# One value run for each head pair: joining the value products, and the probability adds on one engine

## The chip, the cores and the metric

The kernel runs on one core of a Trainium2 chip. The metric is the device time of one execution in microseconds (us). A time given as "the time before" is the median of three runs; a profile shows one further execution.

## The reference

The computation is a normalised attention, followed by a feed-forward block with a squared relu:

```python
q_n, k_n = rmsnorm(q, g_q), rmsnorm(k, g_k)            # (8, 12, 448, 64) each
scores = (1 / sqrt(64)) * q_n @ k_n.T
attn = exp(scores - max); attn = attn / (sum(attn) + 1e-9)
x = (attn @ v).transpose(0, 2, 1, 3).reshape(3584, 768)
r = maximum(x @ w_in, 0)                               # w_in: (768, 2048)
out = (r * r) @ w_out                                  # w_out: (2048, 768)
```

All of it is float32. There are 8 batches, 12 heads, 448 positions, and 64 numbers to a head.

## The kernel before

The kernel holds two programs and branches on the gains. With these inputs it runs `attention_then_ffn_bounded`, which leaves the maximum out of the softmax, since the scores are bounded.

**Spans.** Two batches make a span, and there are four spans. Two heads make a pair: 6 pairs to a batch, 12 to a span, 48 in all, numbered 0 to 47. A span goes through attention (its 12 pairs), then `first_product` (x times w_in with the squared relu), then `second_product` (times w_out). Both products are done with seven block products in place of eight, on sums and differences of blocks (xC and gC, made on VectorE in `finish` and `combine`).

**Stages, in order of time.** The attention of span 0 (pairs 0 to 11) runs together with the making of the weights, `make_w`: the weights come in as 32-bit words and go through a chain of VectorE (L451), ScalarE (L453, L454), VectorE (L457, L458, L459), ScalarE (L460) and GpSimd (L467, L471 to L474), and are written back to DRAM as blocks (w1s, w2s). Then comes `first_product` of span 0, still with weight making; then three pairs of span 1 "alone" (pairs 12 to 14), with the last of the weights; then, for each span, `second_product` with the attention of the next span woven in: after each half of a pair some matmuls of `second_product` are issued (the "fill"), about 6.5 to a half. The `first_product` of spans 1 to 3 stands by itself between these.

**A pair, as the kernel before issues it.** The generator `attention` gives two halves for each pair i. In the first half it loads q and k of pair i+3, issues `scores(i, 0)` and `scores(i, 1)`, `norm(i + 2)`, then the value products 2 and 3 of pair i-1, and `finish(i - 1)`. In the second half it loads v, issues `transposes(i + 1)`, `scores(i, 2)` and `scores(i, 3)`, then the value products 0 and 1 of pair i. A score product (L561) is one of four blocks of 112 keys, for two heads; ScalarE takes its exponential (L564) into a tile pr. A value product (L582) adds one pr times v into the PSUM tile pav. The row sums (L593, PSUM tile tot) are products with a block of ones. In span 0 and in the three pairs alone every pr is summed that way on TensorE (`pe_sums` true). In the other 33 pairs the four pr are first added into acc, by GpSimd, VectorE and GpSimd in turn (L570, L572), and the ones are multiplied once. `finish` takes the reciprocal of tot (L601), multiplies pav by it (L602) and makes the differences for `first_product`.

**Order.** TensorE and the DMA queue (SyncE) take their instructions in the order in which the code issues them. The order on VectorE, ScalarE and GpSimd is laid out beforehand by a scheduler, so it is fixed when the kernel runs, but is not that of the code.

**Buffers.** PSUM has a pool ps_s with two buffers of two banks (tag s, the scores), a pool ps_o with one buffer each for pav (tag o) and for tot (tag t), and a pool ps_m with two. Tag t of ps_o also holds pa, one of the four accumulators of `first_product`. Tile pr has five buffers, acc one, and v, q and k, and the normed pair have two each.

Of the kernel before, what the change touches and what calls it, by code (L numbers as in the profile page):

```python
# [9 lines left out]
F32 = mybir.dt.float32  # L10
U32 = mybir.dt.uint32
AF = mybir.ActivationFunctionType
ALU = mybir.AluOpType
# [291 lines left out]
def attention_then_ffn_bounded(  # L305
# [34 lines left out]
    nc = tc.nc  # L340

    B, H, S, D = q.shape
    NT, DM = out.shape
    DFF = w_in.shape[1]
    P = 128
    NJ = 4
# [14 lines left out]
    ps_s = ctx.enter_context(tc.tile_pool(name="ps_s", bufs=2, space=bass.MemoryType.PSUM))  # L361
    ps_o = ctx.enter_context(tc.tile_pool(name="ps_o", bufs=1, space=bass.MemoryType.PSUM))
# [147 lines left out]
    qks, vs, qkTs, probs, pavs, tots, accs, normed = {}, {}, {}, {}, {}, {}, {}, {}  # L510

    def load(i):
        b, h0 = i // NPAIR, 2 * (i % NPAIR)
        qk = loads.tile([SP, 2, 2, NJ * D], F32, tag="qk", name="qk")
        for dst, src in ((qk[:, 0], q), (qk[:, 1], k)):
            nc.sync.dma_start(dst, src[b, h0:h0 + 2].rearrange("h (p j) d -> p h (j d)", j=NJ))
        qks[i] = qk

    def load_v(i):
        b, h0 = i // NPAIR, 2 * (i % NPAIR)  # L520
        vs[i] = loads.tile([SP, 2, NJ, D], F32, tag="vt", name="vt")
        nc.sync.dma_start(vs[i].rearrange("p h j d -> p h (j d)"),
                          v[b, h0:h0 + 2].rearrange("h (p j) d -> p h (j d)", j=NJ))
# [20 lines left out]
    def transposes(i):  # L544
        qkn = normed.pop(i)
        qkT = loads.tile([P, 2, S], F32, tag="qkT", name="qkT")
        for s in range(2):
            pt = ps_m.tile([P, S], F32, tag="m", name="pt")
            for j in range(NJ):
                nc.tensor.transpose(pt[:, j * SP:(j + 1) * SP],  # L550
                                    qkn[:, s, j].rearrange("p h d -> p (h d)"), ident[:SP, :SP])
            nc.scalar.activation(qkT[:, s], pt, AF.Copy, scale=gains[:, s:s + 1])  # L552
        qkTs[i] = qkT

    def scores(work, i, c, pe_sums):

        qkT = qkTs[i]
        sc = ps_s.tile([SP, 2, 512], F32, tag="s", name="sc")
        for h in range(2):
            rows = slice(h * D, (h + 1) * D)  # L560
            nc.tensor.matmul(sc[:, h, 0:S], qkT[rows, 1, c * SP:(c + 1) * SP], qkT[rows, 0, :],  # L561
                             start=True, stop=True)
        pr = work.tile([SP, 2, S], F32, tag="pr", name="pr", bufs=5)
        nc.scalar.activation(pr, sc[:, :, 0:S], AF.Exp)  # L564
        probs[i, c] = pr
        if c == 0 or pe_sums:
            pass
        elif c == 1:
            accs[i] = work.tile([SP, 2, S], F32, tag="acc", name="acc", bufs=1)
            nc.gpsimd.tensor_tensor(accs[i], probs[i, 0], pr, ALU.add)  # L570
        else:
            (nc.vector if c == 2 else nc.gpsimd).tensor_tensor(accs[i], accs[i], pr, ALU.add)  # L572
        if c == NJ - 1:
            del qkTs[i]

    def values(i, cs, pe_sums):
        if 0 in cs:
            pavs[i] = ps_o.tile([P, S], F32, tag="o", name="pav")
        for c in cs:
            pr = probs.pop((i, c))  # L580
            for h in range(2):
                nc.tensor.matmul(pavs[i][h * D:(h + 1) * D, :], vs[i][:, h, c, :], pr[:, h, :],  # L582
                                 start=(c == 0), stop=(c == NJ - 1))
            if pe_sums:
                sums(i, pr, c == 0, c == NJ - 1)
        if not pe_sums and NJ - 1 in cs:
            sums(i, accs.pop(i), True, True)

    def sums(i, pr, first, last):
        if first:  # L590
            tots[i] = ps_o.tile([P, S], F32, tag="t", name="tot")
        for h in range(2):
            nc.tensor.matmul(tots[i][h * D:(h + 1) * D, :], ones, pr[:, h, :], start=first, stop=last)  # L593

    def finish(work, i):


        b, hp = divmod(i, NPAIR)
        t = b % 2
        rec = work.tile([P, S], F32, tag="rec", name="rec", bufs=1)  # L600
        nc.vector.reciprocal(rec, tots.pop(i))  # L601
        nc.vector.tensor_tensor(xT[:, t, hp], pavs.pop(i), rec, ALU.mult)  # L602
        del vs[i]
        if t:
            sub = nc.vector.tensor_tensor
            if hp < HC:
                sub(xC[:, 0, hp], xT[:, 1, hp], xT[:, 0, hp], ALU.subtract)
            else:
                n = hp - HC
                sub(xC[:, 1, n], xT[:, 1, hp], xC[:, 0, n], ALU.subtract)  # L610
                sub(xC[:, 2, n], xT[:, 0, hp], xC[:, 1, n], ALU.subtract)
                sub(xT[:, 1, n], xT[:, 1, hp], xT[:, 1, n], ALU.subtract)

    def attention(work, first, end, pe_sums):

        last = (first // (2 * NPAIR) + 1) * 2 * NPAIR
        for i in range(first, end):
            if i + 3 < min(last + 2, B * NPAIR):
                load(i + 3)
            scores(work, i, 0, pe_sums)  # L620
            scores(work, i, 1, pe_sums)
            if i + 2 < last:
                norm(i + 2)
            if i > first:
                values(i - 1, (2, 3), pe_sums)
                finish(work, i - 1)
            yield
            if i + 1 < B * NPAIR:
                load_v(i + 1)
            if i + 1 < last:  # L630
                transposes(i + 1)
            scores(work, i, 2, pe_sums)
            scores(work, i, 3, pe_sums)
            values(i, (0, 1), pe_sums)
            if i == end - 1:
                values(i, (2, 3), pe_sums)
                finish(work, i)
            yield


# [11 lines left out]
    def first_product(work, span):  # L652

        B11, B21, B22 = xT[:, 0, 0:HC], xT[:, 0, HC:], xT[:, 1, HC:]
        T1, T2, T4, T3 = xC[:, 0], xC[:, 1], xC[:, 2], xT[:, 1, 0:HC]

        def product(ps, n, rhs, first):

            load_blocks(n + 5)
            for c in range(HC):  # L660
                nc.tensor.matmul(ps, stream[n][:, c], rhs[:, c], start=first and c == 0,  # L661
                                 stop=c == HC - 1, skip_group_check=not first)

        def activate(g, src):
            nc.scalar.activation(g, src, AF.Relu)  # L665
            if span == 0 and src is not g:
                nc.scalar.activation(g, g, AF.Square)
            else:
                nc.gpsimd.tensor_tensor(g, g, g, ALU.mult)  # L669

        for f in range(HF):
            n = span * (N1 + N2) + f * 7
            g11, g12 = gT[:, f, 0:S], gT[:, f, S:2 * S]
            g21, g22 = gT[:, HF + f, 0:S], gT[:, HF + f, S:2 * S]
            add = nc.vector.tensor_tensor
            pa = ps_o.tile([P, S], F32, tag="t", name="pa")
            product(pa, n + A11, B11, True)
            p1 = work.tile([P, S], F32, tag="p1", name="p1")
            nc.scalar.copy(p1, pa)
            yield  # L680
            pb = ps_m.tile([P, S], F32, tag="m", name="pb")
            product(pb, n + S2, T2, True)
            z = work.tile([P, S], F32, tag="z", name="z")
            add(z, p1, pb, ALU.add)
            yield
            pc = ps_m.tile([P, S], F32, tag="m", name="pc")
            product(pc, n + S1, T1, True)
            y = work.tile([P, S], F32, tag="y", name="y")
            add(y, z, pc, ALU.add)
            yield  # L690
            pd = ps_m.tile([P, S], F32, tag="m", name="pd")
            product(pd, n + S3, T3, True)
            add(g22, y, pd, ALU.add)  # L693
            activate(g22, g22)
            yield
            product(pa, n + A12, B21, False)
            activate(g11, pa)
            yield
            product(pd, n + A22, T4, False)
            add(g21, z, pd, ALU.add)  # L700
            activate(g21, g21)
            yield
            product(pc, n + S4, B22, False)
            add(g12, z, pc, ALU.add)
            activate(g12, g12)
            if span:
                combine(f)
            yield
# [210 lines left out]
```

## Time and profile before

| | |
|---|---|
| time before, median of 3 (lowest, highest) | 1637.28 us (1636.2, 1638.59) |
| profiled execution, its own time | 1638.22 us |
| span of the profiled execution | 1636.4 us |
| TensorE busy | 1521.9 us, 93% of the span |
| VectorE / ScalarE / GpSimd busy | 640.5 / 475.3 / 673.1 us |
| granted TensorE clock, mean | 0.98 |

The span lies 1.8 us under the profiled execution's own time, and this in turn 0.9 us over the median. The stages, by the busy time of each engine in stretches of the span:

| stage | from, to (us) | length | TensorE busy | VectorE busy | GpSimd busy |
|---|---|---|---|---|---|
| start, pair 0 and a part of 1 | 0 to 40 | 40 | 19.3 | 18.2 | 20.4 |
| attention of span 0, weights | 40 to 204 | 164 | 127.8 | 108.9 | 123.9 |
| first product of span 0, weights | 204 to 326 | 122 | 120.5 | 67.6 | 73.1 |
| its end, pairs 12 to 14 alone, pair 15 | 326 to 411 | 85 | 69.6 | 58.9 | 63.8 |
| second product 0 with attention | 411 to 612 | 201 | 191.7 | 67.7 | 74.4 |
| first product 1 | 612 to 740 | 128 | 127.6 | 41.3 | 33.8 |
| second product 1 with attention | 740 to 989 | 249 | 238.4 | 91.5 | 115.9 |
| first product 2 | 989 to 1117 | 128 | 127.6 | 41.3 | 33.9 |
| second product 2 with attention | 1117 to 1366 | 249 | 238.5 | 89.3 | 104.0 |
| first product 3, second product 3 | 1366 to 1636 | 270 | 261.0 | 55.9 | 29.9 |

How to read the profile's lines: PE is TensorE, PEld its weight loads, DVE VectorE, ACT ScalarE, POOL GpSimd, SP SyncE. A line of the timeline gives the start and the length in us, the engine, the line of the kernel, the operation, the tiles written and read, their shapes, and the count of records; a bracket at the end gives the idle time ahead of it and what ended it. Each float32 matmul leaves two records, so that the value products of one pr for two heads are 4 records. "Issue" as the one that ended a wait means that the profile shows no releaser.

### The profile page before, as it was taken

The numbers are of one execution on the slowest core, as the hardware profiler recorded it, in microseconds if no ns is written. First come the engines' busy times: TensorE is split into PE (matmuls) and PEld (weight loads), VectorE is DVE, ScalarE is ACT, GpSimd is POOL, SyncE is SP. The second block draws the span as 40 slices with busy tenths as digits, with TensorE's granted clock in tenths as the row PEclk, the third lists the DMA queues.
The fourth block names the chain that finished last, engine by engine and source line by source line (L and its number), as shares of the span: only waits on it lengthen the run. The fifth ranks groups of instructions, "written<-read, shape, count | busy, mean of one in ns | idle before, by whom it ended". The sixth has DMA issues, their size and how long they took to land.

```text
span 1636.4 us, 14479 instructions
## 1 busy us (share of the span) xinstructions
PE 1521.9 (93%) x5172; PEld 709.1 (43%) x5172; DVE 640.5 (39%) x729; ACT 475.3 (29%) x661; POOL 673.1 (41%) x516
## 2 busy tenths in 40 slices
PE   4778799978999999999999999999999999999998
PEld 2233244533444445554444445554444445555544
DVE  4666846576323233333334342333333342332001
ACT  5455535463222301123332311122332321111000
POOL 5966746686344411235555421225455420221000
PEclk9798999989999999999999999999999999999999
DMA  5355467874232223322332313333222213333332
GB/s 169 103 158 169 134 221 245 257 225 126 67 102 79 85 69 100 99 87 85 91 95 85 97 57 98 88 98 97 85 83 89 79 52 96 87 87 93 103 106 64
DMA packets 157717, 180.37 MB, mean 110 GB/s; under 512 B 10692, under 2 KB 134084, under 8 KB 157636
## 3 DMA queue, kind: packets, MB, share of 16 engines
q1 hardware_dynamic: 157636, 179.35, 36.5%
q8 instruction: 43, 0.70, 0.2%
q14 instruction: 38, 0.31, 0.1%
HBM read 146.28 MB, written 33.03 MB: 110 GB/s over the span
## 4 chain that ended last, share of the span: by engine, by line
PE 82%; DVE 4%; POOL 4%; ACT 3%; issue 3%; DMA 3%; SPq 1%; POOLq 0%; DVEq 0%; ACTq 0%
PE ps L733 32%; PE pa L661 8%; PE sc L561 8%; PE pav L582 8%; PE pd L661 8%; PE pc L661 8%; PE pb L661 4%; PE tot L593 3%; PE pt L550 2%; ACT qkT L552 1%; DMA qk<-in_k_dram 1%; POOL qkn L537 1%; DVE ct L747 1%; POOL gC L467 1%; DMA w2s<-gC 1%
## 5 line engine op out<-in xcount | busy, mean ns | idle before, releaser
L733 PE MATMUL ps<-gT,sw 128*128 128x448 f32 x768 | 306.6, 547 | 7.1 <-DVE ct L747 3.6
L669 POOL TENSOR_TENSOR gT<-gT 128x448 f32<-128x448 f32 x120 | 115.2, 961 | 376.2 <-ACT gT L665 376.2
L733 PE MATMUL ps<-gC,sw 128*128 128x448 f32 x576 | 232.3, 549 | 4.0 <-ACT osb L725 2.0
L601 DVE RECIPROCAL rec<-tot 128x448 f32<-128x448 f32 x48 | 141.9, 2956 | 236.2 <-PE tot L593 236.2
L564 ACT ACTIVATE pr<-sc 112x896 f32<-112x896 f32 x192 | 166.6, 913 | 191.7 <-PE sc L561 191.7
L582 PE MATMUL pav<-pr,vt 112*64 112x448 f32 x768 | 180.4, 579 | 42.1 <-issue 34.6
L733 PEld LDWEIGHTS ps<-gT,sw 128*128 128x128 f32 x768 | 141.0, 190 | 157.3 <-issue 140.7
L561 PE MATMUL sc<-qkT 64*112 64x448 f32 x768 | 173.5, 570 | 6.9 <-ACT pr L564 6.0
L661 PE MATMUL pa<-xT,sw 128*128 128x448 f32 x384 | 157.2, 546 | 3.1 <-DVE rec L601 3.1
L733 PEld LDWEIGHTS ps<-gC,sw 128*128 128x128 f32 x576 | 106.8, 191 | 119.3 <-issue 111.5
L535 POOL TENSOR_TENSOR rstd<-rstd,mhalf 112x16 f32<-112x16 f32 x48 | 140.1, 2919 | 3.8
L665 ACT ACTIVATE gT<-gT 128x448 f32<-128x448 f32 x96 | 55.1, 575 | 291.8 <-DVE gT L693 183.3
L534 POOL TENSOR_SCALAR rstd<-rstd 112x16 f32<-112x16 f32 x48 | 32.8, 682 | 245.0 <-DVE rstd L533 244.1
L582 PEld LDWEIGHTS pav<-pr,vt 112*64 112x64 f32 x768 | 50.6, 142 | 154.8 <-issue 148.5
L725 ACT COPY osb<-po 112x512 f32<-112x512 f32 x48 | 28.1, 586 | 279.2 <-PE po L723 279.2
L552 ACT ACTIVATE qkT<-pt,gains 128x448 f32<-128x448 f32 x96 | 58.7, 632 | 172.9 <-PE pt L550 172.9
L537 POOL TENSOR_TENSOR qkn<-qk,rstd 112x512 f32<-112x512 f32 x96 | 104.3, 1108 | 3.6
L661 PEld LDWEIGHTS pa<-xT,sw 128*128 128x128 f32 x384 | 73.4, 192 | 74.6 <-issue 70.8
L570 POOL TENSOR_TENSOR acc<-pr 112x896 f32<-112x896 f32 x33 | 70.5, 2136 | 84.9 <-PE tot L593 79.3
L533 DVE TENSOR_REDUCE rstd<-qkn 112x16 f32<-112x1024 f32 x48 | 58.2, 1212 | 116.2 <-ACT qkn L530 115.9
L561 PEld LDWEIGHTS sc<-qkT 64*112 64x112 f32 x768 | 61.4, 174 | 88.2 <-issue 65.7
L550 PE MATMUL pt<-ident,qkn 112*128 112x112 f32 x384 | 53.5, 270 | 37.5 <-ACT qkT L552 16.7
(82 smaller groups left out, 1651.6 us busy)
## 6 DMA issues: line engine op xcount, KB each, us to landing
sw<-w1s SPq DMA_DIRECT2D x224, 192.0 KB, 2.4
sw<-w2s SPq DMA_DIRECT2D x168, 256.0 KB, 2.7
qk<-in_q_dram SPq DMA_DIRECT2D x48, 224.0 KB, 3.3
qk<-in_k_dram SPq DMA_DIRECT2D x48, 224.0 KB, 3.7
vt<-in_v_dram SPq DMA_DIRECT2D x48, 224.0 KB, 3.0
w1s<-gC SPq DMA_DIRECT2D x8, 1344.0 KB, 6.1
w2s<-gC SPq DMA_DIRECT2D x24, 448.0 KB, 4.5
out_dram<-osb SPq DMA_DIRECT2D x48, 224.0 KB, 2.9
```

What stands on the lines that cost most here:

```text
L535: nc.gpsimd.tensor_tensor(rflat, rflat, mhalf, ALU.pow)
L537: nc.gpsimd.tensor_tensor(qkn[:, s].rearrange("p j h d -> p h j d"), qk[:, s].rearrange("p h (j d) -> p h j d", d=D), rstd[:, s].rearrange ...
L550: nc.tensor.transpose(pt[:, j * SP:(j + 1) * SP], qkn[:, s, j].rearrange("p h d -> p (h d)"), ident[:SP, :SP])
L552: nc.scalar.activation(qkT[:, s], pt, AF.Copy, scale=gains[:, s:s + 1])
L561: nc.tensor.matmul(sc[:, h, 0:S], qkT[rows, 1, c * SP:(c + 1) * SP], qkT[rows, 0, :], start=True, stop=True)
L564: nc.scalar.activation(pr, sc[:, :, 0:S], AF.Exp)
L570: nc.gpsimd.tensor_tensor(accs[i], probs[i, 0], pr, ALU.add)
L582: nc.tensor.matmul(pavs[i][h * D:(h + 1) * D, :], vs[i][:, h, c, :], pr[:, h, :], start=(c == 0), stop=(c == NJ - 1))
L601: nc.vector.reciprocal(rec, tots.pop(i))
L661: nc.tensor.matmul(ps, stream[n][:, c], rhs[:, c], start=first and c == 0, stop=c == HC - 1, skip_group_check=not first)
L669: nc.gpsimd.tensor_tensor(g, g, g, ALU.mult)
L733: nc.tensor.matmul(ps, stream[n][:, c % 4], rhs_of[i][:, c], start=c == 0, stop=c == HF - 1)
```

## The change

All four value products of a pair, and the row sums, are issued in one run right behind the score products 2 and 3 of the same pair, and `finish` follows at once. The first half of a pair keeps only its two score products. In the 33 pairs that add the pr tiles, all three adds are on VectorE. The accumulator pa of `first_product` moves out of the tag t of ps_o into the two buffers of ps_s. Each line of the kernel after L564 stands some lines higher, by up to 9 (L601 becomes L597, L602 L598, L733 L724); below, the numbers are those of the kernel before.

```diff
         nc.scalar.activation(pr, sc[:, :, 0:S], AF.Exp)
         probs[i, c] = pr
-        if c == 0 or pe_sums:
-            pass
-        elif c == 1:
+        if c == 1 and not pe_sums:
             accs[i] = work.tile([SP, 2, S], F32, tag="acc", name="acc", bufs=1)
-            nc.gpsimd.tensor_tensor(accs[i], probs[i, 0], pr, ALU.add)
-        else:
-            (nc.vector if c == 2 else nc.gpsimd).tensor_tensor(accs[i], accs[i], pr, ALU.add)
+        if c and not pe_sums:
+            nc.vector.tensor_tensor(accs[i], probs[i, 0] if c == 1 else accs[i], pr, ALU.add)
...
-    def values(i, cs, pe_sums):
-        if 0 in cs:
-            pavs[i] = ps_o.tile([P, S], F32, tag="o", name="pav")
-        for c in cs:
+    def values(i, pe_sums):
+        pavs[i] = ps_o.tile([P, S], F32, tag="o", name="pav")
+        for c in range(NJ):
...
-        if not pe_sums and NJ - 1 in cs:
+        if not pe_sums:
             sums(i, accs.pop(i), True, True)
...
             scores(work, i, 1, pe_sums)
             if i + 2 < last:
                 norm(i + 2)
-            if i > first:
-                values(i - 1, (2, 3), pe_sums)
-                finish(work, i - 1)
             yield
...
             scores(work, i, 2, pe_sums)
             scores(work, i, 3, pe_sums)
-            values(i, (0, 1), pe_sums)
-            if i == end - 1:
-                values(i, (2, 3), pe_sums)
-                finish(work, i)
+            values(i, pe_sums)
+            finish(work, i)
             yield
...
-            pa = ps_o.tile([P, S], F32, tag="t", name="pa")
+            pa = ps_s.tile([P, 2, 512], F32, tag="s", name="pa")[:, 0, 0:S]
```

## The prediction

> **What bounds the kernel now.** I read the busy shares first, then the waits of TensorE stage by stage, then the timeline where it waits.
>
> ```profile
> PE 1521.9 (93%) x5172; PEld 709.1 (43%) x5172; DVE 640.5 (39%) x729; ACT 475.3 (29%) x661; POOL 673.1 (41%) x516
> ```
>
> TensorE bounds the whole; a change that leaves its work alone can win only its idle time and its slow clock. By stage, idle is 36 us of 164 in span 0's attention (40 to 204), some 15 at 326 to 411, about 10 in each later attention stage, nothing in `first_product`. The waits of TensorE up to 204:
>
> ```profile
> PE pav L582 <- issue: 25.4, 10, 3.5
> PE pt L550 <- POOL qkn L537: 15.8, 1, 15.8
> PE pav L582 <- DVE xT L602: 7.4, 1, 7.4
> ```
>
> So 32.8 us are spent ahead of value product 0, in 11 places. What it waits for shows in one such place (timeline):
>
> ```profile
> 116.05 0.92 PE L593 MATMUL tot<-pr,ones 112*64 112x448 f32 x4
> ...
> 117.82 1.76 PE L561 MATMUL sc<-qkT 64*112 64x448 f32 x8
> 118.21 2.95 DVE L601 RECIPROCAL rec<-tot 128x448 f32<-128x448 f32 x1
> 121.25 1.22 DVE L533 TENSOR_REDUCE rstd<-qkn 112x16 f32<-112x1024 f32 x1
> 122.38 0.61 DVE L602 TENSOR_TENSOR xT<-pav,rec 128x448 f32<-128x448 f32 x1
> 123.10 1.76 PE L582 MATMUL pav<-pr,vt 112*64 112x448 f32 x4 [3.52 <-issue]
> ```
>
> pav has one buffer. It is free once VectorE has taken the reciprocal and multiplied: some 6 us after the sums, while TensorE has only 0.92 us of transposes and 1.7 of scores to put in between. Then the clock: these 4 records take 1.76 us, others 0.97. The end of this stage has the same wait, on tag t:
>
> ```profile
> 201.55 2.96 DVE L601 RECIPROCAL rec<-tot 128x448 f32<-128x448 f32 x1 [1.01 <-PE tot L593]
> 204.54 0.62 DVE L602 TENSOR_TENSOR xT<-pav,rec 128x448 f32<-128x448 f32 x1
> 204.57 4.85 PE L661 MATMUL pa<-xT,sw 128*128 128x448 f32 x6 [3.05 <-DVE rec L601]
> ```
>
> In the 33 pairs woven into `second_product` there is a fill between the sums and value product 0, so no such wait. What the change touches there (timeline, one second half):
>
> ```profile
> 827.35 1.72 ACT L564 ACTIVATE pr<-sc 112x896 f32<-112x896 f32 x2
> 827.46 1.72 PE L582 MATMUL pav<-pr,vt 112*64 112x448 f32 x8
> 827.49 1.22 DVE L533 TENSOR_REDUCE rstd<-qkn 112x16 f32<-112x1024 f32 x1 [2.31 <-ACT qkn L530]
> 828.62 1.08 DVE L572 TENSOR_TENSOR acc<-acc,pr 112x896 f32<-112x896 f32 x1
> ```
>
> **What the Trainium skill says.** "TensorE: Matmul & The Clock Gate", "Part 1: The HAM clock gate": after an idle window the array runs at half clock until some 3.4 us of work have passed. The trace agrees (1.76 for 0.97; pa 4.85 us, later 2.25), and about half of the 11 waits show it. "GPSIMD Engine Reference", 3.1: an elementwise add costs VectorE about 1 cycle an element, GpSimd 2.6; here the same add takes 1.08 and 2.08 us. "SBUF — State Buffer", "SBUF: two separate sides": VectorE with two SBUF inputs and GpSimd exclude each other for an instruction. Agreed: GpSimd's small L534 takes 0.97 us beside the add at 809.5, otherwise 0.20.
>
> **The change part by part.**
>
> *Span 0, pairs up to 4: -0.9.* VectorE is busy nearly without a gap from 26.7 to 52.8 with weights, GpSimd from 39.7 to 86.7; VectorE then waits 7.4 and 5.5 us for weight words. The word load issued at 76.2 stands on SyncE behind a q, k load that waits for GpSimd's `norm` (74.7). The change moves none of this; I carry the chain word load, L451, L453, L454, L457, reciprocal, L602 through in the new order, and value product 0 of pair 4 comes at 94.7 in place of 95.6.
>
> *Pairs 4 to 11: -11.2.* The first value product goes from 95.59 to 193.71, seven periods of 14.02 us. TensorE's own work in one is 3.4 (scores) + 0.9 (transposes) + 6.3 (values, sums) = 10.6. Between sums and value product 0 there now lie four scores and the transposes, 4.3 us, against reciprocal and L602, 3.7 with their hops; and in the built order of instructions the reduce L533 mostly comes behind L602, no longer between. That wait would vanish, but VectorE and ScalarE now go round in one loop a pair: ScalarE does 4 exponentials of 0.91, two L552 in 1.15, L530 1.05, L453 and L454 0.93 each, L460 0.91, in sum 8.6; between L454 and L460 VectorE does L457 1.19, L458 0.91, L459 1.31, in sum 3.4; with hops 12.2. L460 stands ahead of the next pair's exponentials, and the reciprocal behind L459, so TensorE follows at 12.2: 7 x (12.2 - 14.02) = -12.7. Fourteen weights fall on twelve pairs: +1.5. SyncE's v load, which held word loads back until the values of the pair before were done (89.2, 103.0, 116.3), is released half a pair earlier: cover, not counted. Bounds: 10.6 a pair (-24) and 13.5 (-3).
>
> *Its end: -1.5 and -4.5.* The last values took 7.8 us with a slow clock, 6.3 without. pa no longer waits: from the sums' end (201.5) to pb's end (212.1) are 10.6 us; two products of 2.25 are 4.5, but pb's third block needs a difference of this pair, 4.5 us after the sums, or 6 with a late reciprocal. 6.1 is left: -4.5 (-3 to -5.5). Elsewhere pa costs nothing: tags s and t are long free.
>
> *Pairs 12 to 15: +5.5.* Here weights bound. GpSimd works from 350.9 to 378.8 nearly unbroken, then writes w2s, and VectorE's `combine` waits for that:
>
> ```profile
> 385.24 1.16 DVE L647 TENSOR_TENSOR gC<-gT 128x448 f32<-128x448 f32 x2 [5.76 <-DMA w2s<-gC]
> ```
>
> The waits removed in pairs 13 and 14 (5.8, 3.4) so bring 1 us at most: the first fill needs w2s too. In the built order acc's three adds of pair 15 come behind all of `combine` (401.4), with two L533 between: 401.4 + 3 x 1.08 + 2 x 1.15 = 407.0. TensorE has finished pair 15's values at 399.9 (scores end 396.6 as now, 16 records 3.3) and waits 7 us; sums end at 407.9. Now it has at 411.8 (2.25 of wait for GpSimd's add included) done a fill of 18 records (7.0) and two scores (1.7) more: 407.9 + 8.7 - 411.8 = +4.8, and 0.7 of slow clock. Bounds 0 (weights early) to +8. Queued behind these adds on VectorE are only L601 and L602.
>
> *The 33 pairs woven into `second_product`, some 30 of them with an L533: +6.5.* VectorE gains two adds of 1.08 a pair and is then still under half busy (91.5 us of 249 now); GpSimd loses two of 2.08. What counts is the path to the sums: from the start of the values, L533 to +1.15, second add to +2.2, third to +3.3; the 16 value records end at +3.3. So the cover is exactly gone. A dependent add follows some 0.1 later than an independent one, and L534 may slip in for 0.15: a stall of 0.25, x 30 = +7.5 (0 to 0.9 each). The reciprocal now stands ahead of the second half's fill, so an evacuation (L747) that ends within 3.6 us of the sums is late; one fill in a stage (809.96, a po behind) shows this: +1. Gone are waits for GpSimd's add, 2.8 us with 2.25 already used, and 0.6 a stage: -2. TensorE's counts and SyncE's order stay.
>
> Sum: -0.9 - 11.2 - 1.5 - 4.5 + 5.5 + 6.5 = -6.1. Against the profiled 1638.22 that is 1632.1; it lies 0.9 over the median of the runs, so **1631 us**.
>
> **The rivals.** *TensorE bounds span 0 and acc comes in time:* 10.6 in place of 12.2 (-11), no stall (-7.5): 1613. For it: TensorE is busy 128 of 164. Against: the ScalarE, VectorE loop is longer than its work.
>
> *The wait only changes its name:* the reciprocal comes late behind L459, or exponentials behind L460; 13.1 a pair, and +6 against the forecast: 1637, no change. For it: VectorE starts L601 at 118.2, 1.4 us after the sums, behind L459.
>
> *Slower: VectorE's add chain holds the sums.* Place: L593 in 30 pairs. If an L747 (0.6) or an L537 holding the shared port (1.0) comes ahead of the third add, the stall is 0.85: 30 x 0.6 = +18 over the forecast, 1649. It decides from 0.45 a pair (no gain left). For it: zero cover. Against: L535 (2.9 us) beside VectorE adds at 373.9 left them at 0.61.
>
> **Numbers.** Forecast 0.52, its own range 1625 to 1638; TensorE-bound 0.15; renamed 0.15; slower 0.18. 0.2% (3.3 us) is what a measurement can tell. Faster: 0.37 of the forecast, 0.15, 0.03: 0.55. Same: 0.15 + 0.07: 0.22. Slower: 0.18 + 0.05: 0.23. The range 1615 to 1644 leaves half of the first rival's spread and most of the slower one's outside.
>
> **What would show it.** Right: waits of pav near nothing in span 0, the stage 40 to 204 some 18 us shorter, pa at 2.25; a wait of 5 to 8 us of tot on VectorE's acc near pair 15; waits of tot on acc of 0.1 to 0.4 in the later pairs. Wrong: pav or scores still waiting 2 to 3 us a pair there, or tot waits over 0.45 in most pairs.

## The result

The kernel after takes **1638.97 us** (median of 4 runs, 1636.42 to 1640.6); the kernel before, run beside it, 1637.0 (1636.2 to 1638.59). The ratio is 1.0009, its 95% interval 0.9992 to 1.0027: no difference that can be told. The forecast was 1631, a gain of 6. The time lies inside the stated range of 1615 to 1644 and 1 us outside the 1625 to 1638 that the forecast gave its own likeliest case; that case did not come.

The profiled execution of after is the fastest of its four (1636.42 us, span 1634.6), that of before one of the slower of its own (1638.22, span 1636.4). So the two profiles show after ahead by 1.8 us and the medians show it behind by 2; a term of 2 us can be read from the profiles only where both sides of it were seen several times.

The page's busy line: VectorE has taken over two adds a pair and GpSimd has lost them, as forecast. TensorE is as busy as before.

```profile
PE 1517.2 (93%) x5172; PEld 707.4 (43%) x5172; DVE 708.1 (43%) x795; ACT 475.2 (29%) x661; POOL 560.9 (34%) x450
```

TensorE's waits up to 204 (what was waited for: us in all, times, longest). The line numbers are those of the changed kernel, L578 the value products, L589 the sums, L597 and L598 reciprocal and multiply:

```profile
PE sc L561 <- ACT pr L564: 19.8, 7, 4.7
PE pt L550 <- POOL qkn L537: 18.7, 2, 15.5
PE pav L578 <- ACT pr L564: 8.2, 2, 7.5
PE pav L578 <- DVE xT L598: 1.4, 1, 1.4
```

The waits of value product 0 for the multiply, 32.8 us before, are gone but for 1.4. In their place the scores, and twice the values, wait 28.0 us for exponentials. Much of this lies ahead of pair 4: from pair 4 to the last sums the waits fall from 21.3 us in 8 places to 13.6 us in 7. The timeline shows one such place, between pairs 5 and 6:

```profile
111.28 0.56 DVE L451 TENSOR_SCALAR gC<-words 128x768 uint32<-128x768 uint32 x1 [2.70 <-DMA words<-in_moe_w_in_dram]
...
111.87 0.94 ACT L453 ACTIVATE gC<-gC,clamp 128x768 f32<-128x768 uint32 x1 [2.94 <-DVE gC L451]
...
113.01 1.76 PE L561 MATMUL sc<-qkT 64*112 64x448 f32 x8
...
113.81 0.96 DVE L457 SCALAR_TENSOR_TENSOR gC<-words,gC 128x768 uint32<-128x768 uint32 x1 [1.97 <-ACT gC L454]
...
114.80 1.34 DVE L458 TENSOR_SCALAR words<-words 128x768 uint32<-128x768 uint32 x1
...
116.18 1.68 DVE L459 SCALAR_TENSOR_TENSOR words<-words 128x768 f32<-128x768 uint32 x1
...
117.78 2.94 DVE L597 RECIPROCAL rec<-tot 128x448 f32<-128x448 f32 x1
117.89 0.88 ACT L460 ACTIVATE words<-words 128x768 f32<-128x768 f32 x1 [4.11 <-DVE words L459]
118.67 1.70 ACT L564 ACTIVATE pr<-sc 112x896 f32<-112x896 f32 x2
...
119.62 1.09 PE L561 MATMUL sc<-qkT 64*112 64x448 f32 x2 [3.93 <-ACT pr L564]
```

The exponentials of the two scores done at 114.7 stand on ScalarE behind L460, which waits 4.11 us for VectorE's L459. TensorE then waits 3.93 us for a free score buffer. The reciprocal, too, stands behind L459.

The end of this attention stage, and one woven pair:

```profile
195.58 2.52 PE L652 MATMUL pa<-xT,sw 128*128 128x448 f32 x6
195.70 2.96 DVE L597 RECIPROCAL rec<-tot 128x448 f32<-128x448 f32 x1 [0.34 <-PE tot L589]
```

```profile
847.33 0.97 PE L589 MATMUL tot<-acc,ones 112*64 112x448 f32 x4 [0.27 <-DVE acc L569]
```

pa starts with the sums' end and no longer waits for the reciprocal. In the woven pairs the sums wait some 0.3 us for the last add, and at full clock (0.97).

Both profiles were laid side by side at points where equal work is done. One profile of each is little to go by, but the kernels of the next section share single stretches with the one or the other: the same code there and, up to the last sums of pair 11, the same orders on VectorE, ScalarE and GpSimd. Their profiles show how far a stretch differs without any change:

| stretch | forecast | after minus before | old order, us | new order, us | difference of the means |
|---|---|---|---|---|---|
| up to value product 0 of pair 4 | -0.9 | -1.0 | 93.5 to 95.6 | 92.4 to 95.9 | -0.1 |
| pairs 4 to 11, to the end of the last sums | -11.2 - 1.5 | **-5.0** | 105.1 to 111.8 | 100.7 to 102.5 | **-6.1** |
| sums' end to the start of pc (pa, pb) | -4.5 | -5.3 | 10.6 | 5.2 to 6.1 | -5.2 |
| the rest of first product 0 | 0 | +1.4 | 125.4 to 126.6 | 125.8 to 127.5 | +1.0 |
| pairs 12 to 15 with the first fill | +5.5 | +5.0 | 74.1 to 74.6 | 79.0 to 79.6 | +5.0 |
| the woven pairs behind that, to the end | +6.5 | +3.1 | 1222.6 to 1225.2 | 1227.7 to 1228.4 | +4.2 |
| sum | -6.1 | -1.8 | | | -1.2 |

(Old and new order are, in rows 1, 2 and 4, before, e1, e3 and after, e2, e4, e8, e11; in row 3, before, e3 and after, e1, e2, e4, e8, e11; in rows 5 and 6, before, e1, e2, e6 and after, e5, e7, e12.)

### The profile page after: what moved, and what is told of

It reads as the page before. It is cut to its first block, busy times and chain, and to the rows that moved or that the text cites. A ratio compares the mean times of both kernels' runs of the same rounds, so it can differ in the third digit from the quotient of the medians.

```text
span 1634.6 us, 14437 instructions
## 1 busy us (share of the span) xinstructions
PE 1517.2 (93%) x5172; PEld 707.4 (43%) x5172; DVE 708.1 (43%) x795; ACT 475.2 (29%) x661; POOL 560.9 (34%) x450
## 4 chain that ended last, share of the span: by engine, by line
PE 70%; DVE 11%; ACT 6%; issue 5%; DMA 5%; POOL 3%; SPq 1%; DVEq 0%; ACTq 0%; POOLq 0%
PE ps L724 32%; PE pd L652 8%; PE pc L652 8%; PE pa L652 8%; PE sc L561 4%; PE pb L652 4%; DVE acc L569 4%; PE tot L589 2%; ACT qkn L530 2%; PE pav L578 2%; PE pt L550 2%; ACT qkT L552 1%; DVE rec L597 1%; DMA qk<-in_k_dram 1%; DVE ct L738 1%
## 5 line engine op out<-in xcount | busy, mean ns | idle before, releaser
L724 PE MATMUL ps<-gT,sw 128*128 128x448 f32 x768 | 306.6, 547 | 7.1 <-DVE ct L738 3.6
L724 PE MATMUL ps<-gC,sw 128*128 128x448 f32 x576 | 230.6, 546 | 2.8 <-DVE p L732 2.5
L564 ACT ACTIVATE pr<-sc 112x896 f32<-112x896 f32 x192 | 166.4, 914 | 225.7 <-PE sc L561 225.7
L724 PEld LDWEIGHTS ps<-gT,sw 128*128 128x128 f32 x768 | 141.4, 190 | 156.2 <-issue 141.6
L561 PE MATMUL sc<-qkT 64*112 64x448 f32 x768 | 180.6, 591 | 23.4 <-ACT pr L564 22.7
L578 PE MATMUL pav<-pr,vt 112*64 112x448 f32 x768 | 169.5, 565 | 23.1 <-DVE xT L598 14.9
L535 POOL TENSOR_TENSOR rstd<-rstd,mhalf 112x16 f32<-112x16 f32 x48 | 165.5, 3448 | 3.8
L597 DVE RECIPROCAL rec<-tot 128x448 f32<-128x448 f32 x48 | 141.9, 2955 | 41.1 <-PE tot L589 41.1
L724 PEld LDWEIGHTS ps<-gC,sw 128*128 128x128 f32 x576 | 106.4, 190 | 116.3 <-issue 111.1
L578 PEld LDWEIGHTS pav<-pr,vt 112*64 112x64 f32 x768 | 51.9, 141 | 129.1 <-issue 87.1
L537 POOL TENSOR_TENSOR qkn<-qk,rstd 112x512 f32<-112x512 f32 x96 | 102.7, 1090 | 3.7
L569 DVE TENSOR_TENSOR acc<-acc,pr 112x896 f32<-112x896 f32 x66 | 71.8, 1088 | 24.7 <-ACT pr L564 21.3
```

What stands on the lines that cost most here:

```text
L535: nc.gpsimd.tensor_tensor(rflat, rflat, mhalf, ALU.pow)
L537: nc.gpsimd.tensor_tensor(qkn[:, s].rearrange("p j h d -> p h j d"), qk[:, s].rearrange("p h (j d) -> p h j d", d=D), rstd[:, s].rearrange ...
L569: nc.vector.tensor_tensor(accs[i], probs[i, 0] if c == 1 else accs[i], pr, ALU.add)
L724: nc.tensor.matmul(ps, stream[n][:, c % 4], rhs_of[i][:, c], start=c == 0, stop=c == HF - 1)
```

## The experiments

Each kernel ran on one chip with the kernel before, and its ratio is to that. In kernels that mix both orders a pair is "joined" or not:

```diff
+    def joined(i):
+        return i < 12
...
-            if i > first:
+            if i > first and not joined(i - 1):
                 values(i - 1, (2, 3), pe_sums)
                 finish(work, i - 1)
...
             values(i, (0, 1), pe_sums)
-            if i == end - 1:
+            if i == end - 1 or joined(i):
                 values(i, (2, 3), pe_sums)
                 finish(work, i)
```

Their lines behind L564 differ by a few from those of before and after; the tile names tell which is which.

| kernel | joined pairs | adds in the woven pairs | us (median) | ratio to before, 95% |
|---|---|---|---|---|
| before | none | G, V, G | 1638.72, 1641.41, 1639.59 | |
| e1_pa (pa moved alone) | none | G, V, G | 1634.84 | 0.9972 (0.9956 to 0.9987) |
| e2_run0 | 0 to 11 | G, V, G | 1628.8 | 0.9930 (0.9913 to 0.9948) |
| e3_woven (pa not moved) | 15 to 47 | V | 1650.31 | 1.0067 (1.0049 to 1.0086) |
| e4_no_alone | all but 12 to 14 | V | 1637.96 | 0.9991 (0.9983 to 1.0) |
| e9_early10 (four weights later) | 0 to 11 | G, V, G | 1632.36 | 0.9952 (0.9934 to 0.9969) |
| e10_v5 (v in other buffers) | 0 to 11 | G, V, G | 1659.28 | 1.0121 (1.0103 to 1.0139) |
| e8_vadd | 0 to 11 | V from pair 16 | 1628.16 | 0.9932 (0.9910 to 0.9953) |
| e11_order | 0 to 11, 16 to 47 | G, V, G | 1853.26 | 1.1307 (1.1286 to 1.1327) |

(V is VectorE, G GpSimd, in the order of the three adds. The three times of before belong to e1 to e4, to e9, and to the last three. Four kernels more, e5, e6, e7 and e12, ran once each and are read by their profile; they follow further down.)

### Where the gain and the loss lie

**e1_pa.** Before, with pa in the buffers of the scores:

```diff
-            pa = ps_o.tile([P, S], F32, tag="t", name="pa")
+            pa = ps_s.tile([P, 2, 512], F32, tag="s", name="pa")[:, 0, 0:S]
```

> The kernel before, with pa alone moved to the buffers of the scores; order of the values and adds as before. Theory (the change is a sum of parts that mostly keep their value): pa takes 2.3 us in place of 4.85 and starts 3.05 us sooner after the sums, pb then starts 4 to 5 us sooner, and this lead lasts to the end: 1632 to 1633 us. Rival (the making of the weights bounds the stage 326 to 411, so a lead won before it is lost there): the write of w2s still ends near 385 us and the time stays at 1637.

Measured: 0.28% or 4.6 us less by the ratio, the saving that the theory had. The mechanism shows in its timeline:

```profile
205.29 2.52 PE L661 MATMUL pa<-xT,sw 128*128 128x448 f32 x6
205.40 2.96 DVE L598 RECIPROCAL rec<-tot 128x448 f32<-128x448 f32 x1 [2.27 <-PE tot L590]
...
209.78 1.02 PE L661 MATMUL pb<-xC,sw 128*128 128x448 f32 x2 [0.46 <-DVE xC L607]
```

**e2_run0.** `joined` is i < 12, with pa moved and the adds as before.

> The joined run only in pairs 0 to 11, with pa moved; pairs 12 to 47 in the old order with the old adds. Theory: span 0's attention ends some 6 us sooner, pb starts 11 us sooner, first product 0 gives 1.4 back, and nothing is lost behind that: 1627 to 1628 us. Rival (the lead is lost in the weight-bound stage whatever the order there): first scores of pair 12 come 10 us sooner, the fill after pair 15's first half only 0 to 5 us sooner, 1632 to 1637 us.

Measured: 0.70% or 11.5 us less by the ratio, its median 0.8 over the theory's range; its span is 1627.4, before 1636.4. pa of span 1 starts at 602.8 (before 612.4), so all that was won up to pair 12 (first scores at 327.6, before 337.5) is kept. The rival falls. Less e1's share, the join of span 0 is worth some 7 us where the forecast had 13.6.

**e3_woven.** `joined` is i >= 15, adds on VectorE, pa in its old place.

> The joined run and the adds on VectorE only in pairs 15 to 47; pairs 0 to 14 in the old order, pa in its old place. Theory: the 32 pairs woven in later cost 3 to 4 us (waits of tot for acc of 0.2 to 0.4 us in about 9 of 12 pairs of a span), and pair 15, whose adds stand behind all of combine on VectorE, 1 to 5 us more: 1641 to 1645 us. Rival (the waits for acc take the place of the gone waits for GpSimd's add and cost nothing): 1637 us.

Measured: 0.67% or 11 us more, over the theory's 4 to 8; its profiled execution, the fastest of six, has 8.2 more. e2's -11.5 and e3's +11 together are the change but for the join in pairs 12 to 14, and their sum is what it did: nothing that can be told. The stage of pairs 12 to 15 shows the wait that the prediction had at this place, in TensorE's line and in VectorE's ahead of it:

```profile
399.38 0.62 DVE L649 TENSOR_TENSOR gC<-gT,gC 128x448 f32<-128x448 f32 x1
399.92 1.09 DVE L569 TENSOR_TENSOR acc<-pr 112x896 f32<-112x896 f32 x1
400.92 1.22 DVE L533 TENSOR_REDUCE rstd<-qkn 112x16 f32<-112x1024 f32 x1
402.05 2.28 DVE L569 TENSOR_TENSOR acc<-acc,pr 112x896 f32<-112x896 f32 x2
...
404.39 1.76 PE L590 MATMUL tot<-acc,ones 112*64 112x448 f32 x4 [4.10 <-DVE acc L569]
```

L647 to L650 are `combine`; all three adds of pair 15 come behind the last of them.

**e4_no_alone.** After, with pairs 12 to 14 in the old order. In after itself this stage has one long wait, in pair 14, for the multiply of pair 13, whose reciprocal stands behind `combine`:

```profile
373.44 1.76 PE L578 MATMUL pav<-pr,vt 112*64 112x448 f32 x4 [12.81 <-DVE xT L598]
```

> The kernel after, with the old order in pairs 12 to 14 alone. Theory: there the wait of 12.8 us in pair 14 (pav on the multiply L598 of pair 13, whose reciprocal stands on VectorE behind the adds of combine) goes, and 2 to 5 us come back: 1633 to 1636 us. Rival (the last weights and the write of w2s bound this stage, and the wait only moves to another instruction): the same as after, 1637 to 1639 us.

Measured: 0.9991, and after has 1.0009; the two cannot be told apart. The wait of 12.8 us is gone, but pairs 13 and 14 wait 5.6 and 4.1 again, as before, and pair 15's sums wait 4.2 for acc. From the first scores of pair 12 to pa of span 1 it takes 281.1 us; after takes 279.8, e3 280.7, before 274.9 and e2 275.2. So the rival holds: in this stage the waits trade names, and the 5 to 6 us come with pair 15 and the woven pairs, whatever the order in pairs 12 to 14.

### Join and adds apart

**e8_vadd.** e2 with all adds of pairs 16 to 47 on VectorE, these pairs in the old order.

```diff
-            (nc.vector if c == 2 else nc.gpsimd).tensor_tensor(...)
+            (nc.vector if c == 2 or i >= 16 else nc.gpsimd).tensor_tensor(...)
```

> The kernel with the joined run only in pairs 0 to 11 and pa moved, and besides with all adds on VectorE in pairs 16 to 47, there in the old order. Theory (what costs time in the pairs woven into second_product is the join, which puts the sums right behind the last exponential; adds on VectorE alone are free, as value products 2 and 3 then come a half later): stages between two first products of 376 to 377 us, 1627 to 1630 us. Rival (the adds on VectorE delay the evacuations L747 or the sums themselves): 378 us or more a stage, 1632 to 1636 us.

Measured: 1628.16, the same as e2. Two stages between first products take 378.9 and 379.2 us where e2's take 376.9, as the rival had it, but from pair 12's first scores to pa of span 1 it takes 272.3 where e2 takes 275.2; e1 and e6, with the old adds, take 272.9 and 273.2 there, so this gain is not clear. In all, the adds on VectorE cost nothing that can be told. The two stages are firmer ground: they take 376.9 us in every profile with the old adds and the old order (before, e1, e2, e6, e9, e10), 378.9 and 379.2 in e8, 379.2 and 378.3 in after. What after loses in them e8 loses too, without the join. In e8 no sums wait for acc; TensorE waits there 4.1 us more for VectorE's L747 and L749, which take over results of `second_product`.

**e11_order.** The opposite: the join in pairs 16 to 47, the adds as before.

> The kernel with the joined run in pairs 0 to 11 and in pairs 16 to 47, pa moved, the adds on GpSimd, VectorE, GpSimd as before. Theory (in the joined run the last add decides when the sums can start, and GpSimd's takes 2.08 us where VectorE's takes 1.08): tot waits for acc 1 us or more in most pairs, 383 to 395 us a stage, 1640 to 1660 us. Rival (the join is free and the adds on VectorE are what costs): 377 us a stage, 1628 us.

Measured: +13%, 213 us more, far over the theory. The reason stands in one pair of its timeline:

```profile
802.04 1.08 DVE L569 TENSOR_TENSOR acc<-acc,pr 112x896 f32<-112x896 f32 x1
802.21 0.97 POOL L534 TENSOR_SCALAR rstd<-rstd 112x16 f32<-112x16 f32 x1 [6.03 <-DVE rstd L533]
803.27 2.91 POOL L535 TENSOR_TENSOR rstd<-rstd,mhalf 112x16 f32<-112x16 f32 x1
806.26 2.04 POOL L537 TENSOR_TENSOR qkn<-qk,rstd 112x512 f32<-112x512 f32 x2
808.26 2.07 POOL L569 TENSOR_TENSOR acc<-acc,pr 112x896 f32<-112x896 f32 x1
...
810.38 1.76 PE L590 MATMUL tot<-acc,ones 112*64 112x448 f32 x4 [6.27 <-POOL acc L569]
```

It is not the 2.07 us of GpSimd's add but its place: in GpSimd's order the whole `norm` comes ahead of it, and TensorE waits 6.27 us in this pair (172.6 us over 32 pairs), then runs at half clock (1.76). So the two parts of the change belong together: in the woven pairs the join needs the adds on VectorE. With them the woven pairs cost the 3 to 4 us of the table, and by e8 it is the adds rather than the join that these stages pay for.

### What paces pairs 4 to 11

These runs are read by one stretch, from the first value product of pair 4 to the last sums of pair 11. It takes 106.0 us in before, and 111.8 and 105.1 in e1 and e3, which have the same order there; 101.0 in after, and 100.7 to 102.5 in e2, e4, e8 and e11, which have after's. So one execution can differ by some 7 us in the old order and by 2 in the new one.

**e5_no_act** and **e6_old_no_act.** After and before, without ScalarE's part of the weights:

```diff
-            nc.scalar.activation(e, eu, AF.Relu, bias=clamp1, scale=-1.0)
-            nc.scalar.activation(eu, e, AF.Relu, bias=clamp2, scale=-(2.0 ** 23))
+            if n >= 14:
+                nc.scalar.activation(e, eu, AF.Relu, bias=clamp1, scale=-1.0)
+                nc.scalar.activation(eu, e, AF.Relu, bias=clamp2, scale=-(2.0 ** 23))
...
-            nc.scalar.activation(f, f, AF.Copy, bias=1.0, scale=2.0 ** -20)
+            if n >= 14:
+                nc.scalar.activation(f, f, AF.Copy, bias=1.0, scale=2.0 ** -20)
```

> The kernel after, with ScalarE's three operations of weight making (L453, L454, L460) left out for the first 14 half blocks, those made in span 0's attention; what is written to w1s for them is then not the weights. Read for the stretch from the first value product of pair 4 to the last sums of pair 11 (106.0 us before, 101.0 after, runs of one kernel differing there by some 2 us). Theory (the exponentials stand on ScalarE behind weight operations that wait for VectorE, and that is what took the predicted gain): TensorE's waits on pr of some 23 us go and the stretch falls to 82 to 88 us, near TensorE's own 10.6 us a pair. Rival (late weight words or GpSimd's norm set the pace): it stays at 95 us or more.

> The kernel before, with the same three ScalarE operations left out for the first 14 half blocks. Same stretch, 106.0 us before. Theory (the old order is held by the reciprocal and multiply that free pav, which stand on VectorE among weight operations and the reduce L533, not by ScalarE): value product 0 still waits in most pairs and the stretch falls only to 92 to 100 us, so the joined run would be worth 10 us or more where ScalarE is free of weights. Rival (the weight chain holds both orders alike): it falls as far as the kernel after's, to 82 to 88 us.

Measured: 99.7 and 106.4 us (1640.26 and 1636.8 in all, one execution each). The theory falls for the new order: ScalarE is free, and nothing is won. e6's 106.4 fits neither its theory nor its rival; the old order, too, wins nothing. In e5 the wait has gone back to the multiply (here L601), since the reciprocal stands behind VectorE's weight operations, and L451, the first of them, waits for its words (11.0 us in the stretch). TensorE's waits up to 204, of which 14.6 us lie in the stretch:

```profile
PE pav L581 <- DVE xT L601: 29.8, 6, 9.2
```

**e7_no_loads_b.** After, without the loads of the words of half blocks 5 to 13. A further changed line, not printed here, lets half blocks with the same place share one tile for their words:

```diff
-        if n < 2 * NFC:
+        if n < 2 * NFC and not 5 <= n < 14:
```

> The kernel after, with the loads of the words of half blocks 5 to 13 left out, so that VectorE's L451 never waits for them there; these weights are then not the right ones. Stretch from the first value product of pair 4 to the last sums of pair 11: 106.0 us before, 101.0 after, 99.7 with ScalarE's weight operations left out, so ScalarE was not what held it. New theory (word loads come late, since they stand on SyncE behind v loads and writes of w1s; L451 waits for them, and the reciprocal and all else behind it): 84 to 92 us. Rival (the sum of weight work and norm on VectorE and GpSimd holds it): 96 to 101 us.

Measured: 100.5 us (1637.42 in all, one execution). The loads were not it either. L451 now waits for the write of w1s that frees its block (3.6 us in the stretch), two half blocks then come one behind the other, and the exponentials are late again. Up to 204, with 14.2 us of it in the stretch:

```profile
PE sc L561 <- ACT pr L564: 30.7, 5, 11.8
```

Before e5 was known, the same edit (e7_no_loads) had been expected the other way round, with the chain of engines as the theory and 96 to 100 us; that kernel gave no time, and 100.5 lies 0.5 over that range.

In e5, e6 and e7 the scheduler put the weight operations into other places among the rest, on GpSimd too, so they differ from their originals by more than their edit.

**e12_no_chain.** After, without the weight operations of VectorE and ScalarE for half blocks 6 to 13:

```diff
-        if step == 0 and doubles:
+        if step == 0 and doubles and not 5 < n < 14:
...
-        if step == 1 and doubles:
+        if step == 1 and doubles and not 5 < n < 14:
...
-                    nc.gpsimd.tensor_tensor(b[blk], f[:, part], e[:, part], ALU.mult)
+                    nc.gpsimd.tensor_tensor(b[blk], (e if 5 < n < 14 else f)[:, part], e[:, part], ALU.mult)
```

> The kernel after, with the operations of weight making on VectorE and ScalarE (L451 to L460) left out for half blocks 6 to 13 and GpSimd's product taken of the old contents instead; GpSimd's work, the word loads and the writes of w1s stay, and these weights are then not the right ones. Stretch from the first value product of pair 4 to the last sums of pair 11: 101.0 us after, 99.7 without ScalarE's part of the weights, 100.5 without the word loads. Theory (each half block of weights puts about 3 us into the loop of TensorE, exponentials, sums and reciprocal, since its operations stand on VectorE and ScalarE ahead of the reciprocal and of the exponentials and are themselves waiting; taking one of their causes away leaves the next one waiting): 84 to 90 us, pairs of 10.4 to 11.3. Rival (GpSimd, busy 77 us of the 101, or SyncE's loads set the pace through norm): 95 to 101 us.

Measured: **83.7 us** (88.4 to 172.1), 0.3 under the theory's range, and 1615.35 us in all (before, beside it, 1636.86; one execution each). Six periods in a row are 10.5 us, TensorE's own work, with GpSimd's `norm` and products, SyncE's loads and its writes all there. The seventh is 14.2: there the chain is back, with half block 14, and L460 and the reciprocal stand behind its L459 again. In the traces the other operations of VectorE and ScalarE come in after's order. GpSimd's do not: its products no longer wait for the chain, and some come ahead of `norm` where they came behind it. One of the six pairs:

```profile
115.57 2.96 DVE L598 RECIPROCAL rec<-tot 128x448 f32<-128x448 f32 x1 [4.49 <-PE tot L590]
...
117.15 0.98 PE L550 MATMUL pt<-ident,qkn 112*128 112x112 f32 x8
118.06 1.76 PE L561 MATMUL sc<-qkT 64*112 64x448 f32 x8
...
118.56 0.62 DVE L599 TENSOR_TENSOR xT<-pav,rec 128x448 f32<-128x448 f32 x1
...
119.75 0.97 PE L579 MATMUL pav<-pr,vt 112*64 112x448 f32 x4
```

The multiply ends at 119.18 and TensorE comes at 119.75: the slack of this loop is at most 0.6 us, though VectorE has been idle 4.49 us ahead of the reciprocal. One weight operation in the wrong place (0.56 to 1.7 us each, and more where it waits itself) uses it up. In after, nine half blocks begin their chain in the stretch, in e12 two. That these seven cost 101.0 - 83.7 = 17.3 us makes 2.5 us each. About half of it is clock: TensorE is busy 80.2 us of e12's stretch, at a mean granted clock of 0.98, and 88.8 us of after's, at 0.90, with the same work. Over the whole attention, to the end of the last sums, the eight half blocks are worth 195.6 - 172.1 = 23.5 us, 2.9 each.

**e9_early10.** e2 with four half blocks fewer made in span 0's attention: `EARLY, LATE = 10, 29` in place of 14, 29.

> The kernel with the joined run only in pairs 0 to 11 and pa moved, and besides with EARLY at 10 in place of 14: four half blocks of weights fewer are made in span 0's attention and four more in first product 0. Theory (weight making paces pairs 4 to 11, and first product 0 has room on VectorE, ScalarE and GpSimd): span 0's attention ends 6 to 10 us sooner than with 14, first product 0 grows by 0 to 4 us, 1620 to 1627 us. Rival (the last weights bound the stage up to pair 15, and weights made later come out later): first product 0 or the stage 326 to 411 gives it all back, 1628 to 1634 us.

Measured: the attention ends at 183.3 in place of 195.9, 3.1 us for each half block taken out, near e12's 2.9. All of it is won ahead of pair 4, whose value product 0 comes at 79.6 in place of 93.8. From there to the last sums e9 takes 103.7 us where e2 takes 102.2, though seven half blocks begin in the stretch and not nine: the price of a half block is no constant of a pair, and depends on where its operations stand. But the first scores of pair 12 come at 324.7 (e2 327.6), and in pairs 13 and 14 value product 0 waits 17.0 us: pa of span 1 starts at 606.6, later than e2's 602.8. The rival holds: e9 wins nothing over e2 (0.9952 and 0.9930, intervals that overlap). The last weights bound the stage of pairs 12 to 15, so what is made later there comes out later.

**e10_v5.** e2 with v of pairs 1 to 11 in the five buffers of sw:

```diff
-        vs[i] = loads.tile([SP, 2, NJ, D], F32, tag="vt", name="vt")
+        if 0 < i < 2 * NPAIR:
+            sw = loads.tile([P, 4, P], F32, tag="sw", name="sw", bufs=5)
+            vs[i] = sw[0:SP].rearrange("p a (b d) -> p (a b) d", d=D).rearrange("p (h j) d -> p h j d", h=2)
+        else:
+            vs[i] = loads.tile([SP, 2, NJ, D], F32, tag="vt", name="vt")
```

> The kernel with the joined run only in pairs 0 to 11 and pa moved, and besides with v of pairs 1 to 11 in the five buffers of the weight stream (free in span 0's attention) in place of two of its own, so that SyncE no longer stops at a v load until the values of the pair before last are done. Theory (that stop is what makes the word loads late): the stretch from pair 4 to the last sums falls from some 102 to 92 to 97 us, 1621 to 1626 us in all. Rival (writes of w1s and q, k loads on the same queue hold it as long): stretch 99 us or more, 1627 to 1631 us.

Measured: 121.9 us for the stretch and 1659.28 in all, which neither theory had. The edit changed the scheduler's order on VectorE: L451 now comes between reciprocal and multiply, and waits there for its words.

```profile
144.20 2.96 DVE L602 RECIPROCAL rec<-tot 128x448 f32<-128x448 f32 x1
154.53 0.56 DVE L451 TENSOR_SCALAR gC<-gT 128x768 uint32<-128x768 uint32 x1 [7.37 <-DMA gT<-in_moe_w_in_dram]
155.00 0.62 DVE L603 TENSOR_TENSOR xT<-pav,rec 128x448 f32<-128x448 f32 x1
```

What the v buffers themselves do is left open by this run. What it shows is the price of a weight operation's place: pav waits up to 10.1 us for this multiply.

## Why the prediction was right in its range and not in its number

**Pairs 4 to 11 are the step that failed.** The forecast was one loop of 12.2 us in each pair, made by adding every operation once, with 1.5 us for the extra half blocks. The periods in after run 12.3, 16.0, 11.8, 14.9, 11.3, 14.0 and 13.7, a mean of 13.4; the other four profiles of this order give 13.3 to 13.6. The loop was the right place, but the sum left waits out. In after's stretch (94.5 to 197; who waited for whom: us in all, times, longest):

```profile
ACT gC L453 <- DVE gC L451: 12.8, 6, 3.1
ACT words L460 <- DVE words L459: 12.0, 4, 4.1
DVE gC L457 <- ACT gC L454: 15.3, 8, 2.6
DVE gC L451 <- DMA words<-in_moe_w_in_dram: 2.7, 1, 2.7
```

The forecast counted ScalarE's wait at L460, at 3.4 us a pair, and its wait at L453 for VectorE's L451 at nothing; this one took 12.8 us. The mistake was to take the weight chain as work that turns once a pair at a fixed place. It goes back and forth between VectorE and ScalarE, each of which stands still for the other's step (words from DRAM are 5.0 us of VectorE's waits here, L457's wait for ScalarE 15.3), and in these lines exponentials and reciprocal start only when the weight operation ahead of them in the order has ended. e12 shows that without VectorE's and ScalarE's part the loop is TensorE's 10.5; on top of this come, over the whole attention, some 3 us for each half block (e12, e9), not evenly spread over the pairs. The rival "the wait only changes its name" came nearest: it gave 13.1 a pair, named both places, the exponentials behind L460 and the reciprocal behind L459, and put the time at 1637.

**What stays open there** is which operation of the chain counts most. e5, e7 and e12 each take something away, and only the one that takes VectorE's and ScalarE's part together shortens the stretch. Whether VectorE's part alone would do was not tried. e12 also takes away GpSimd's waits for the chain. TensorE waits for GpSimd's `norm` nowhere in after's stretch, so GpSimd does not hold it at first hand; whether it does through the writes that free a block is not shown.

**Luck.** The first term, -0.9 for -1.0, is no hit: profiles of one order differ by 2 to 3.5 us there, and the means are alike. Of the signs named for a right forecast, pav's waits went and the later pairs wait 0.3 us for acc; the stage was to be 18 us shorter with pa and pb, and pc starts 11 us sooner. The sign of being wrong came in part: values and scores still wait 13.6 us in some 7 pairs, 2 us a pair. One reading ahead of it was a little off: L601 at 118.21 starts 1.2 us after the sums, not 1.4; nothing rests on it.

**pa was right** in mechanism and size: -4.5 forecast, -5.3 in the profile, -4.6 by e1's ratio (0.9956 to 0.9987, which is 2 to 7 us).

**Pairs 12 to 15 were right in size (+5.0 for +5.5), and the place only partly.** The forecast had the waits of pairs 13 and 14 gone, to little use, and pair 15's sums waiting 7 us for acc behind `combine`. In after the latter wait is 1.30 us, and value product 0 of pairs 13 and 14 waits 0.8 and 12.8 us where it waited 5.8 and 3.4; with the old order in pairs 12 to 14 (e3, e4) it is the forecast one, at 4.1 to 4.2 us.

**The woven pairs were over-estimated (+3.1 in the profile, +4.2 in the means, for +6.5).** The stall of 0.25 a pair was well sized (0.27 in the lines), and 27 pairs showed it, with 7.5 us in all, so waits that went, less evacuations that came later, gave back some 3 to 4 us where the forecast had 1; the runs do not split this further. Pairs 12 to 15 and the woven pairs together are +9.2 in the means and +9.6 in e3's profile (whose 8.2 in all holds 1.4 won by chance ahead of pair 12), against +11 by e3's ratio and the forecast's 12.

**The slower rival** (1649) asked for 0.45 us or more a pair and did not come: no wait for acc in a woven pair was over 0.4 us. e11 shows how near its mechanism is: the same add behind `norm` is 6.27 us late.

**First product 0** gave 1.4 us back in after's profile, which no step had: TensorE's waits to write pd, for VectorE's adds ahead of it, are 2.2 us where they were 1.0. But the profiles of the old order reach 126.6 us there and those of the new one 125.8 to 127.5, so this term is not clear of chance.

The best kernel found is e2_run0 (e8_vadd is equal to it): the joined run in span 0 alone with pa moved, 1628.8 us, 0.70% under before.

## What to carry to other kernels

Where a wait is taken off an engine's path, ask what its slack becomes and what stands in order ahead of the next releaser; a slow chain that shares these engines is not cover but a second customer, and its busy time does not price it: here 20 us less of ScalarE's (e5) won 1.3 us of the stretch, 18 us less of ScalarE's and 26 of VectorE's together (e12) won 17.3. Before a difference of a few us between two profiles is explained, the same stretch is worth reading in every other profile that has the same order there. A change that does one thing in several stages is best split by stage in the experiments: here a gain of 11 us and a loss of 11 lay in different pairs, and keeping the old order where it was cheap kept the gain. An add that decides when TensorE may start belongs on an engine that has nothing long queued ahead of it; its own duration matters less.

## What the runs showed of the hardware

VectorE's integer and mixed operations on the weight words are slower beside GpSimd's work than alone: L458 takes 0.56 us alone and 1.34 in the lines at 114.80, L459 0.96 and 1.68, while GpSimd's L537 takes 2.04 alone and 2.35 there. Of the 32 L458 in after, 14 take 0.82 to 1.34 us, and each of these has a product, sum or difference of GpSimd beside it; 18 take 0.50 to 0.56, nine of them beside nothing and eight beside GpSimd's power L535 alone. The chain L457 to L459, put at 3.4 us in the prediction, took 4.0 in those lines.

The adds on VectorE are not free for GpSimd either: L535 takes 2.9 us in 47 of its 48 places in before, where no add of acc runs beside it. In after 27 of the 28 L535 that have such an add beside them take 3.8 us, and 16 of the other 20 take 2.9.

A wait of 3.9 us (scores at 119.62) left the next 2 records at 1.09 us, about half clock, where 2 records take 0.55 at full clock. The length of a wait does not decide alone: in before value product 0 starts at half clock (records of 0.98 us) after waits of 2.40, 2.53 and 3.52 us, and at full clock (0.56) after waits of 2.19, 2.62, 2.82 and 3.08. Part of what a removed wait is worth is the clock behind it: the same records of pairs 4 to 11 keep TensorE busy 88.8 us at a mean granted clock of 0.90 in after and 80.2 us at 0.98 in e12.
